# Five seven-product pairs in one more group of a fused linear-attention and SwiGLU kernel, batch 7's q in fewer early steps, and the last copy in another tile

## The chip, the cores and the metric

The kernel runs on one core of a Trainium2 chip. The core has a matrix engine (TensorE, in the profile PE, with its weight loads as PEld), a vector engine (VectorE, DVE), an engine for functions of single elements (ScalarE, ACT), a general one (GpSimd, POOL), and one that mostly starts transfers (SyncE, SP). They run side by side, each through its own list of instructions in order, and wait for each other through semaphores. The metric is the device time of one execution in microseconds (us): lower is better. Matmul results go to PSUM, which has eight banks of 128 partitions x 512 numbers of 32 bits; the kernel calls them pG (two), pV (three) and pX (three). Everything else on the chip lies in SBUF.

## The reference

q, k and v have 8 batches, 8 heads, 576 positions and 64 dimensions. The first half is linear attention, the second a SwiGLU block on its output x (4608 tokens of 512):

```python
def phi(x):
    return np.where(x > 0, x, np.exp(x) - 1.0) + 1.0
q_p, k_p = (phi(q), phi(k))
kv = np.einsum('bhsd,bhse->bhde', k_p, v)
z = np.sum(k_p, axis=2)
num = np.einsum('bhsd,bhde->bhse', q_p, kv)
den = np.einsum('bhsd,bhd->bhs', q_p, z)[..., None] + 1e-06
x = (num / den).transpose(0, 2, 1, 3).reshape(B * S, H * D)
g = x @ w_gate                       # 512 to 1536
out = (g / (1 + np.exp(-g)) * (x @ w_val)) @ w_out   # and back to 512
```

## The kernel before, in words

**Groups.** A batch is 9 units of 64 tokens, so there are 72 units; a group is 8 units, 512 tokens, and there are 9 groups, 0 to 8. Since a group has 8 units and a batch 9, group g needs the end of batch g-1 and most of batch g. Group 0 and the attention of batches 0 to 2 run in a part of their own ahead of line 800. From there the work of groups 1 to 8 is recorded as a list of operations: each call of op(engine, cost, function, reads, writes) appends one. At the end the line numbers of a long string, steps, say in which order the recorded operations are issued. The order was found beforehand by a planner from the costs given to op and the named reads and writes; the kernel itself only plays it back. So the order on each engine is fixed, and semaphores are set from the tiles and banks that instructions touch.

**Attention, for each batch b.** phis (line 913) makes phi(x) as min(exp(x), max(x, 0) + 1): for k and for q, plus_1_all (line 132) writes max + 1 of the whole tile into kp or qp on VectorE, ScalarE puts exp into a tile ek or eq (exp_, line 122), and least (line 138) takes the minimum with it. Two table loads of ScalarE stand around it. casts copies v; kv_prd (line 926, in ORDER the letter J) multiplies k and v; chain (line 882) spreads the sums z over all partitions (zb, zb_copy) and calls norm (line 888), which normalizes q in qp in place, in chunks of units: s3_prod, s3_half, s3_reduce, s3_recip and s3_scale on VectorE (lines 224 to 250). Then tr transposes the chunk by a DMA into qT. S3 and SCALE say which chunks are done right after chain, S3L and SCALEL which are left to the next group's first layer. x_prd (line 932, the letter M) makes x of the next group from qT and the k-v product, in four banks that x_copy moves to SBUF.

**First layer of group g** (layer_1, line 1028). The 1536 hidden columns are 12 blocks. A plain block is c_chunk (line 822): 16 matmuls for two blocks (8 for gate, 8 for value over four slices of x, each 128x128 by 128x512), a silu on ScalarE and one multiplication on VectorE for each block. A pair, pair_prd (line 837), makes two blocks by Winograd's form of Strassen's scheme: 7 products of half-size matrices instead of 8, each of four matmuls with 256 columns (prd_1, line 342). It needs sums of weights, made once (wl_sum, the list WL says in which group), and sums of x, made for each group (x_sums). Between the products ScalarE copies three partial results (keep_1, line 365) and applies silu twice (silu_1, line 368), and VectorE does two multiplications and an addition from PSUM (lines 371 and 857) and one multiplication in SBUF (line 866). NP says how many pairs a group has: 0, 3, 3, 5, 5, 6, 6, 6 for groups 1 to 8. With four pairs or more, layer_1 interleaves two pairs and fills the places between their products with what the second layer of the group before left over (fill) and with the chunks of the plain blocks.

**Second layer** (layer_2, line 1099) uses the same 7-product scheme over the whole layer: products 1 to 7 for two token halves (prd, line 439; h_sum, line 419, on VectorE makes the sums). The string ORDER[g] gives the products in order; what stands behind the bar | is left to the next group's first layer. keep, fin and copy_half bring the results to osb, and put sends them out. In the last group, the last product's bank pX_1 is emptied by two engines, partitions 0 to 63 by VectorE and 64 to 127 by ScalarE (lines 1000 and 1002), both into the tile osb_3, and two transfers follow.

Of the kernel before, what the change touches and what calls it, by code (L numbers as in the profile page):

```python
# [9 lines left out]
AF = mybir.ActivationFunctionType  # L10
# [7 lines left out]
def kernel(  # L18
# [215 lines left out]
    def s3_reduce(b, c):  # L234
        j0, j1 = js_of(c)
        nc.vector.tensor_reduce(out=den[:, HL * j0:HL * j1],
                                in_=prod[:, 0:j1 - j0, :].rearrange("p j (l d) -> p (j l) d", d=D)[:, :, 0:D // 2],
                                axis=AX.X, op=ALU.add)
# [581 lines left out]
    NP = {1: 0, 2: 3, 3: 3, 4: 5, 5: 5, 6: 6, 7: 6, 8: 6}  # L820
# [60 lines left out]

    def chain(b):
        op("PE", 0.25, lambda: zb(b), [f"R{b % 2}.{hh}" for hh in range(2)], ["X0"])
        for hh in range(2):
            op("ACT", 0.3, lambda hh=hh: zb_copy(b, hh), ["X0"], [f"zbc{hh}"])
        norm(b, S3[b], SCALE[b])

    def norm(b, chunks, scales):
        dens = []
        for (j0, j1) in chunks:  # L890
            (c, n, js) = ((j0, j1), j1 - j0, list(range(j0, j1)))
            dens.append(f"den{c}")
            op("DVE", 0.07 + 0.147 * n, lambda c=c: s3_prod(b, c), rqp(b, js) + ["zbc0", "zbc1"], ["prod"])
            op("DVE", 0.07 + 0.069 * n, lambda c=c: s3_half(c), ["prod"], ["prod"])
            op("DVE", 0.08 + 0.143 * n, lambda c=c: s3_reduce(b, c), ["prod"], [f"den{c}"])
# [16 lines left out]

    def phis(b):
        op("ACT", 1.28, lambda: nc.scalar.preload_act_table_set("exp_and_others"), [], ["table"])
        for (src, e, dst, w) in ((k16, ek, kp, [["kp1.0"], ["kp1.1"]]), (q16, eq, qp, [rqp(b, lps=[0]), rqp(b, lps=[1])])):
            a = "k" if src is k16 else "q"
            we = [["ek0.0", "ek0.1"], ["ek1.0", "ek1.1"]] if src is k16 else [["eq0"], ["eq1"]]
# [6 lines left out]
    KVB = {**{b: ["X2", "V2"] for b in range(B)}, 2: ["X0", "X1"], 7: ["X1", "V0"], 6: ["X1", "V0"], 5: ["X1", "V0"]}  # L924
# [34 lines left out]
    def l2_prd(g, n, tt, fs=tuple(range(HF)), done=True):  # L959
# [37 lines left out]
        if n == 4:  # L997
            if last and tt:
# [3 lines left out]
                op("ACT", 0.3, lambda: nc.scalar.activation(out=o2[hi, 0:HD], in_=x[hi, 0:HD], func=AF.Copy, bias=0.0,  # L1002
                                                            scale=1.0 / SC), [nm(x)], [f"o{2 + tt}.0b"])
                op("SP", 0.06, lambda: put_1(g, tt, 1, 0, 0, nc.sync), [f"o{2 + tt}.0a"], [])
                op("ACT", 0.06, lambda: put_1(g, tt, 1, 0, 1, nc.scalar), [f"o{2 + tt}.0b"], [])
# [14 lines left out]
    def put_1(g, tt, th, ch, e, eng):  # L1020
        (b, j) = units(g)[2 * (2 * th + tt) + e]
        eng.dma_start(out=out[S * b:S * b + S, HD * ch:HD * ch + HD].rearrange("(c j) f -> j c f", j=J)[j],  # L1022
                      in_=osb[2 * th + tt][C * e:C * e + C, HD * ch:HD * ch + HD])
# [73 lines left out]
    WL = {2: [(1, 1, 1), (2, 0, 1)], 3: [(2, 1, 1), (3, 0, 1)], 4: [(3, 1, 1)]}  # L1097
# [45 lines left out]
    ORDER[99] = ""; S3[7], SCALE[7], S3L[7], SCALEL[7] = ((0, 1),), ((0, 1),), ((1, 5), (5, 9)), ((1, 3), (3, 6), (6, 9)); S3[6], SCALE[6], S3L[6], SCALEL[6] = ((0, 2),), ((0, 2),), ((2, 5), (5, 9)), ((2, 5), (5, 9),); S3[5], SCALE[5], S3L[5], SCALEL[5] = ((0, 5),), ((0, 3), (3, 5)), ((5, 9),), ((5, 9),)  # L1143

    ORDER.update({g: "10 11 20 21 60 61 50 51 70 71 M 30 31 | 41 40 J" for g in (3,4)})
# [3 lines left out]
    def program():  # L1149
# [21 lines left out]
        0 1 4 14 15 9 17 18 10 5 20 21 23 6 24 26 27 16 29 2 19 30 32 8 3 33 35 36 7 22 38 28 41 25 39 40 42 31  # L1171
        34 44 171 45 43 47 37 63 49 46 64 48 66 12 50 67 69 105 65 70 51 11 72 52 73 75 68 71 13 76 106 78 74 77
        79 53 81 82 80 84 83 54 85 107 87 55 88 86 90 89 91 119 93 92 94 96 114 95 97 56 99 98 100 102 57 101
        103 113 127 108 58 104 129 128 109 131 115 110 133 59 130 135 117 132 60 134 137 111 139 136 125 138 112
        120 141 143 118 140 145 142 116 122 147 146 150 124 148 126 144 153 151 162 121 154 165 123 156 155 168
        61 163 176 157 158 177 62 149 169 172 152 164 179 167 170 166 159 178 160 181 197 161 180 199 342 183
        200 182 343 198 202 184 204 201 206 173 203 207 185 209 205 208 211 210 214 186 215 174 212 218 220 219
        222 175 221 216 223 213 225 187 224 227 217 229 226 188 230 228 285 232 231 189 234 236 235 237 233 240
        242 238 241 245 243 246 239 248 190 247 250 244 249 252 251 253 276 255 193 254 257 256 259 277 258 191
        260 262 261 264 192 194 267 265 268 263 271 266 273 269 272 274 270 284 298 275 300 278 280 299 302 288  # L1180
        281 279 304 282 301 306 286 303 308 305 283 310 296 309 307 312 287 311 314 289 313 293 316 290 318 317
        291 315 321 319 294 324 297 333 322 326 292 336 325 195 334 339 328 329 327 347 196 320 504 323 335 348
        340 330 337 350 341 338 332 349 352 331 368 353 370 354 369 371 355 373 372 375 356 295 377 357 378 380
        379 351 382 381 358 385 386 376 383 389 344 387 391 393 374 392 394 390 384 396 359 398 395 388 400 399
        360 401 397 403 456 402 405 404 407 345 408 406 411 409 413 346 412 361 416 410 414 417 419 415 418 421
        364 423 422 424 420 426 425 447 428 362 427 430 429 431 448 363 365 433 432 435 438 436 439 434 442 437
        444 440 443 445 441 455 469 446 471 449 451 470 473 459 452 450 475 474 472 477 453 457 479 476 454 478
        481 467 480 462 483 460 485 458 482 487 484 486 464 461 489 498 488 491 468 463 501 490 499 492 494 505
        493 502 507 465 506 510 495 508 512 466 496 497 515 366 517 516 523 513 367 500 503 509 518 525 514 519
        511 527 529 524 528 540 526 542 541 545 543 531 547 546 629 550 530 552 548 551 554 532 553 556 544 558  # L1190
        555 561 557 559 563 562 549 566 560 564 568 567 570 565 569 533 572 571 574 520 577 620 579 575 578 582
        580 573 584 534 583 586 588 585 587 590 576 593 535 595 581 594 591 598 589 600 596 599 602 601 592 603
        536 606 521 608 611 604 537 607 612 522 609 605 614 613 615 617 597 616 618 610 628 622 642 619 644 623
        643 624 646 632 621 648 625 647 645 650 627 637 652 649 626 654 651 653 635 656 633 658 700 657 660 655
        538 630 662 659 539 661 671 663 701 640 631 674 664 666 672 677 667 665 673 679 675 678 702 682 676 680
        684 668 639 681 669 687 670 689 634 688 703 694 641 685 636 690 696 686 691 683 698 638 706 695 715 699
        697 717 704 716 720 708 722 721 725 718 705 707 727 726 723 729 728 709 731 730 719 733 736 710 732 734
        738 737 724 741 735 739 743 742 745 711 747 740 744 746 749 748 752 795 754 750 753 757 796 759 755 758
        761 712 760 763 762 751 765 713 768 764 770 756 769 714 773 766 692 775 871 777 776 778 767 781 771 774
        783 779 782 786 693 784 787 789 809 790 780 788 792 791 793 785 803 815 772 794 817 797 816 819 799 810  # L1200
        798 821 800 820 818 823 801 805 825 822 827 824 802 826 812 829 804 831 872 828 806 833 830 807 832 835
        834 844 873 836 808 847 837 845 839 850 840 838 846 852 848 874 851 849 855 853 842 857 856 841 854 875
        814 860 843 862 876 861 813 865 863 867 877 864 858 869 811 866 859 882 891 868 870 893 892 880 896 883
        898 897 901 894 884 903 902 899 905 904 907 885 906 895 909 912 878 908 914 913 917 900 879 881 910 919
        918 921 915 920 923 922 911 925 928 886 924 926 930 929 916 933 931 927 935 934 937 887 932 939 936 938
        941 940 888 944 942 946 945 949 889 947 951 890 950 953 979 952 955 954 943 957 980 960 956 958 962 961
        965 948 959 968 963 969 966 971 970 972 967 974 964 973 975 977 981 978 976 989 990 991 992 993 983 996
        982 998 1000 997 1002 984 1004 987 999 1011 995 1003 1001 1013 985 1015 988 1014 1012 986 1017 994 1047
        1019 1016 1018 1007 1006 1021 1020 1005 1023 1022 1008 1026 1024 1028 1010 1027 1025 1009 1031 1029 1033
        1048 1032 1030 1049 1036 1034 1038 1037 1035 1050 1041 1039 1051 1043 1042 1040 1052 1045 1044 1060 1046  # L1210
        1062 1061 1065 1063 1067 1066 1053 1070 1064 1068 1072 1071 1074 1069 1076 1073 1075 1078 1077 1054 1081
# [45 lines left out]
```

## Time and profile before

Time: 295.01 us, the median of 3 runs (294.98 to 295.08). The profiled execution spans 293.5 us, with the full TensorE clock throughout.

| what | busy us | share of the span |
|---|---|---|
| TensorE matmuls | 286.2 | 98% |
| TensorE weight loads | 213.0 | 73% |
| VectorE | 258.6 | 88% |
| ScalarE | 236.2 | 80% |
| GpSimd | 45.1 | 15% |

Busy time is the union of an engine's instructions, so that two which overlap by a few hundredths are counted once. A share is an average over the span: the first 20 us, in which data come in and batch 0 is prepared, and the last 4 us, in which results go out, look unlike the rest. In the profile's slices, each digit is the busy share in tenths of a fortieth of the span (7.3 us). A row of a group gives the line, the engine, the operation and its tiles, how often it came, its busy time and the mean of one in ns. A row of the timeline begins with start and duration; in brackets stands how long the engine was idle before it and who ended that.

Groups 1 to 8 run from 52.4 to 289.6 us. A table by stretches, cut where each group's second layer begins, is shown in the prediction.

### The profile page before, as it was taken

The page shows a single profiled execution, that of the slowest core. Times are in us where ns is not written, and L with a number is a line of the kernel's source. Part 1 is how long each engine was busy: PE and PEld are TensorE (multiplying, and loading weights), DVE is VectorE, ACT ScalarE, POOL GpSimd, SP SyncE. Part 2 cuts the span into 40 slices and gives each one's busy share as a digit, 9 for nine tenths or more (in the row PEclk, how much of TensorE's full clock was granted, in tenths as well). Part 3 has the DMA queues.
Part 4 walks back from the last instruction along what each step waited for, and adds up shares of the span by engine and source line. Part 5 has one row for each costly group of instructions (what it writes and reads, how often), then busy time and mean ns, then how long its engine had stood idle before and what let it go on. Part 6 is the DMA issues. An engine that isn't in the chain of part 4 may idle for free.

```text
span 293.5 us, 7371 instructions
## 1 busy us (share of the span) xinstructions
PE 286.2 (98%) x2939; PEld 213.0 (73%) x2939; DVE 258.6 (88%) x521; ACT 236.2 (80%) x406; POOL 45.1 (15%) x59
## 2 busy tenths in 40 slices
PE   7899999999999999999999999999999999999994
PEld 5644454444876687667888788878888888788883
DVE  4766789999999999999979999999999999957982
ACT  4873977993999588987999999999986689669841
POOL 8654436500111001010100111000000000000003
PEclk9999999999999999999999999999999999999999
DMA  7999999995398229853990749701430143033005
GB/s 211 193 196 200 205 208 208 191 229 85 63 175 186 49 54 152 183 75 63 137 179 21 107 65 249 68 3 44 101 65 9 44 109 69 0 68 79 0 2 143
DMA packets 41314, 32.92 MB, mean 112 GB/s; under 512 B 16432, under 2 KB 36592, under 8 KB 41280
## 3 DMA queue, kind: packets, MB, share of 16 engines
q0 software_dynamic: 20304, 18.62, 41.4%
q1 hardware_dynamic: 20736, 13.64, 21.3%
q8 instruction: 23, 0.38, 0.5%
q10 hardware_dynamic: 240, 0.20, 0.3%
q14 instruction: 11, 0.09, 0.1%
HBM read 37.75 MB, written 9.44 MB: 161 GB/s over the span
## 4 chain that ended last, share of the span: by engine, by line
PE 95%; DMA 2%; ACT 1%; issue 0%; DVE 0%; POOL 0%; POOLq 0%
PE pX L456 20%; PE pV L351 14%; PE pG L351 12%; PE pX L351 10%; PE pV L828 8%; PE pG L828 7%; PE pV L456 5%; PE pX L297 3%; PE pV L297 3%; DMA q<-in_q_dram 2%; PE pG L383 2%; PE pV L383 2%; PE pG L297 2%; PE pX L828 2%; PE pX L187 1%; PE pX L268 1%
## 5 line engine op out<-in xcount | busy, mean ns | idle before, releaser
L351 PEld LDWEIGHTS <-wl 128*128 128x128 f16 x414 | 40.2, 98 | 9.4
L456 PEld LDWEIGHTS <-hs 128*128 128x128 f16 x384 | 37.2, 98 | 5.1 <-issue 0.6
L456 PEld LDWEIGHTS <-hT 128*128 128x128 f16 x288 | 27.7, 98 | 5.0 <-DVE hs L425 0.4
L351 PEld LDWEIGHTS <-wg 128*128 128x128 f16 x272 | 26.4, 98 | 5.7
L456 PE MATMUL pX<-ws,hs 128*128 128x256 f16 x240 | 29.1, 273 | 0.0
L828 PE MATMUL pV<-xt,wv 128*128 128x512 f16 x104 | 28.3, 379 | 0.0
L368 ACT ACTIVATE ek<-eq 128x512 f16<-128x512 f32 x34 | 21.3, 625 | 5.1 <-DVE eq L857 5.0
L351 PE MATMUL pV<-xt,wg 128*128 128x256 f16 x168 | 23.9, 273 | 0.0
L368 ACT ACTIVATE ek<-pV 128x512 f16<-128x512 f32 x34 | 20.4, 599 | 3.3 <-PE pV L351 2.6
L828 PE MATMUL pG<-xt,wg 128*128 128x512 f16 x80 | 22.5, 379 | 0.0
L465 ACT ACTIVATE part<-pX 128x256 f32<-128x256 f32 x40 | 14.5, 386 | 6.9 <-PE pX L456 6.7
L351 PE MATMUL pX<-xs,wl 128*128 128x256 f16 x132 | 19.8, 273 | 0.0
L1022 POOL DMA_DIRECT2D out_dram<-osb x5 | 2.7, 541 | 110.5 <-DVE osb L472 110.5
L371 DVE SCALAR_TENSOR_TENSOR r<-pG,rr 128x512 f16<-128x512 f32 x20 | 13.8, 688 | 6.6 <-PE pG L351 6.4
L456 PE MATMUL pX<-wo,hT 128*128 128x256 f16 x138 | 18.2, 273 | 0.0
L374 DVE SCALAR_TENSOR_TENSOR hT<-pV,sil 128x512 f16<-128x512 f32 x26 | 17.5, 682 | 0.5 <-PE pV L828 0.4
L425 DVE TENSOR_TENSOR hs<-hT 128x512 f16<-128x512 f16 (+3 forms) x35 | 17.7, 514 | 0.1
L365 ACT ACTIVATE rr<-pX 128x512 f32<-128x512 f32 x27 | 15.9, 597 | 2.0 <-PE pX L351 1.9
L249 DVE TENSOR_TENSOR qp<-qp,rden 128x768 f16<-128x768 f16 (+3 forms) x19 | 17.2, 906 | 0.0
L828 PEld LDWEIGHTS <-wv 128*128 128x128 f16 x112 | 11.0, 98 | 8.5
L124 ACT ACTIVATE ek<-k 128x1152 f16<-128x1152 f16 x14 | 16.2, 1164 | 1.1 <-DMA k<-in_k_dram 1.0
L351 PE MATMUL pG<-xs,wl 128*128 128x256 f16 x100 | 16.9, 272 | 0.0
(190 smaller groups left out, 723.4 us busy)
## 6 DMA issues: line engine op xcount, KB each, us to landing
out_dram<-osb SPq DMA_DIRECT2D x64, 128.0 KB, 2.4
k<-in_k_dram POOLq DMA_DIRECT2D x7, 576.0 KB, 7.6
q<-in_q_dram POOLq DMA_DIRECT2D x7, 576.0 KB, 10.1
v<-in_v_dram POOLq DMA_DIRECT2D x7, 576.0 KB, 6.4
wg<-in_moe_w_gate_dram POOLq DMA_DIRECT2D x5, 256.0 KB, 9.3
wv<-in_moe_w_val_dram POOLq DMA_DIRECT2D x5, 256.0 KB, 9.9
wo<-in_moe_w_out_dram POOLq DMA_DIRECT2D x2, 512.0 KB, 15.1
ws<-in_k_dram SPq DMA_DIRECT2D x1, 576.0 KB, 3.8
```

Of the source, the lines that this page charges most:

```text
L124: nc.scalar.activation(out=e[:, s, :], in_=src[ix(b)][:, s, :], func=AF.Exp, bias=0.0, scale=1.0)
L249: nc.vector.tensor_tensor(out=qv, in0=qv, in1=rden[:, HL * j0:HL * j1].unsqueeze(2).to_broadcast([P, HL * (j1 - j0), D]), op=ALU.mult)
L297: nc.tensor.matmul(out=ps[:, :], lhsT=src[:, i, P * fb:P * fb + P], rhs=xT[i][g % 2][:, :], start=(i == 0), stop=(i == 3))
L351: nc.tensor.matmul(out=dst[:, HN * e:HN * e + HN], lhsT=lhs, rhs=rhs, start=(n in (1, 5) and e == 0 and c == 0), stop=(c == 1), skip_group ...
L365: nc.scalar.activation(out=dst, in_=halves(src), func=AF.Copy, bias=0.0, scale=scale)
L368: nc.scalar.activation(out=dst, in_=src, func=AF.Silu, bias=0.0, scale=1.0)
L371: nc.vector.scalar_tensor_tensor(out=dst, in0=halves(src), scalar=SC, in1=b, op0=ALU.mult, op1=op1)
L374: nc.vector.scalar_tensor_tensor(out=hT[:, fb, :], in0=pv[:, :], scalar=SC, in1=s[:, :], op0=ALU.mult, op1=ALU.mult)
L425: (eng or nc.vector).tensor_tensor(out=o, in0=a, in1=b, op=op)
L456: nc.tensor.matmul(out=(z if n in (2, 3, 5) else x)[:, 0:HD], lhsT=left(f), rhs=right(f), start=(i == 0 and fs[0] == 0 and (n in (1, 5) or ...
L465: nc.scalar.activation(out=part[:, 2 * i + tt, :], in_=(x if from_x else z)[:, 0:HD], func=AF.Copy, bias=0.0, scale=1.0 / SC)
L828: nc.tensor.matmul(out=dst[:, :], lhsT=src[:, i, P * fb:P * fb + P], rhs=xT[i][g % 2][:, :], start=(i == 0), stop=(i == 3))
```

## The change

It does four things.

1. Group 3 has five pairs instead of three. For that, four of the five late weight sums come in group 2 and one in group 3, group 2's second layer takes the order of groups 3 and 4 (M earlier, and 41 40 J behind the bar), batch 4's k-v product gets the banks X1 and V0 as the later ones have, and the normalization of batches 4 and 5 is cut into other chunks.
2. For batch 7, phis leaves out q's part on VectorE. ScalarE writes exp(q) straight into qp (exp_in), and norm calls q_fin, which makes max(q, 0) + 1 in place in q16 and takes the minimum of both into qp, for unit 0 in group 6 and for units 1 to 8 in group 7.
3. In the last group, ScalarE's copy of the last product goes into the tile part, and is sent from there, so that it doesn't share osb_3 with VectorE's.
4. The order of steps is planned anew.

HALF is a switch that stays on, so that the normalization's steps stay as they were. The diff, with the string of step numbers left out:

```diff
-    def s3_reduce(b, c):
+    def s3_reduce(b, c, d):
...
-    NP = {1: 0, 2: 3, 3: 3, 4: 5, 5: 5, 6: 6, 7: 6, 8: 6}
+    NP = {1: 0, 2: 3, 3: 5, 4: 5, 5: 5, 6: 6, 7: 6, 8: 6}
...
+    HALF = {0: 1}
...
     def norm(b, chunks, scales):
         dens = []
+        if b in LATE:
+            q_fin(b, chunks[0][0], chunks[-1][1])
...
+    LATE = {7: True}
+
+    def exp_in(b, lp):
+        nc.scalar.activation(out=qp[b % 2][:, :, P * lp:P * lp + P].rearrange("p j (s d) -> p s j d", d=D),
+                             in_=q16[ix(b)][:, 2 * lp:2 * lp + 2, :].rearrange("p s (j d) -> p s j d", d=D), func=AF.Exp, bias=0.0,
+                             scale=1.0)
+
+    def q_fin(b, j0, j1):
+        n, js = j1 - j0, list(range(j0, j1))
+        r = q16[ix(b)][:, :, D * j0:D * j1]
+        op("DVE", 0.08 + 0.067 * n, lambda: nc.vector.tensor_scalar(out=r, in0=r, scalar1=0.0, scalar2=1.0, op0=ALU.max, op1=ALU.add),
+           ["q16"], ["q16"])
+        d = qp[b % 2][:, j0:j1, :].rearrange("p j (s d) -> p j s d", d=D)
+        op("DVE", 0.08 + 0.134 * n, lambda: nc.vector.tensor_tensor(out=d, in0=d, in1=r.rearrange("p s (j d) -> p j s d", d=D), op=ALU.min),
+           ["q16"] + rqp(b, js), rqp(b, js))
...
             a = "k" if src is k16 else "q"
+            if a == "q" and b in LATE:
+                for lp in range(2):
+                    op("ACT", 1.07, lambda lp=lp: exp_in(b, lp), ["q16", "table"], w[lp])
+                continue
...
-    KVB = {**{b: ["X2", "V2"] for b in range(B)}, 2: ["X0", "X1"], 7: ["X1", "V0"], 6: ["X1", "V0"], 5: ["X1", "V0"]}
+    KVB = {**{b: ["X2", "V2"] for b in range(B)}, 2: ["X0", "X1"], 7: ["X1", "V0"], 6: ["X1", "V0"], 5: ["X1", "V0"], 4: ["X1", "V0"]}
...
-                op("ACT", 0.3, lambda: nc.scalar.activation(out=o2[hi, 0:HD], in_=x[hi, 0:HD], func=AF.Copy, bias=0.0,
-                                                            scale=1.0 / SC), [nm(x)], [f"o{2 + tt}.0b"])
+                op("ACT", 0.3, lambda: nc.scalar.activation(out=part[hi, 0, :], in_=x[hi, 0:HD], func=AF.Copy, bias=0.0,
+                                                            scale=1.0 / SC), [nm(x)], ["part00"])
                 op("SP", 0.06, lambda: put_1(g, tt, 1, 0, 0, nc.sync), [f"o{2 + tt}.0a"], [])
-                op("ACT", 0.06, lambda: put_1(g, tt, 1, 0, 1, nc.scalar), [f"o{2 + tt}.0b"], [])
+                op("ACT", 0.06, lambda: put_1(g, tt, 1, 0, 1, nc.scalar, part[hi, 0, :]), ["part00"], [])
...
-    WL = {2: [(1, 1, 1), (2, 0, 1)], 3: [(2, 1, 1), (3, 0, 1)], 4: [(3, 1, 1)]}
+    WL = {2: [(1, 1, 1), (2, 0, 1), (2, 1, 1), (3, 0, 1)], 3: [(3, 1, 1)]}
...
-    S3[5], SCALE[5], S3L[5], SCALEL[5] = ((0, 5),), ((0, 3), (3, 5)), ((5, 9),), ((5, 9),)
+    S3[5], SCALE[5], S3L[5], SCALEL[5] = ((0, 3),), ((0, 3),), ((3, 6), (6, 9)), ((3, 6), (6, 9))
+    S3[4], SCALE[4], S3L[4], SCALEL[4] = ((0, 5),), ((0, 3), (3, 5)), ((5, 9),), ((5, 9),)
...
-    ORDER.update({g: "10 11 20 21 60 61 50 51 70 71 M 30 31 | 41 40 J" for g in (3,4)})
+    ORDER.update({g: "10 11 20 21 60 61 50 51 70 71 M 30 31 | 41 40 J" for g in (2,3,4)})
```

## The prediction, as put on record

> **What bounds the kernel now.** I read the busy shares first, then the slices, then the chain that ended last.
>
> ```profile
> PE 286.2 (98%) x2939; PEld 213.0 (73%) x2939; DVE 258.6 (88%) x521; ACT 236.2 (80%) x406; POOL 45.1 (15%) x59
> PE   7899999999999999999999999999999999999994
> DVE  4766789999999999999979999999999999957982
> ACT  4873977993999588987999999999986689669841
> PE 95%; DMA 2%; ACT 1%; issue 0%; DVE 0%; POOL 0%; POOLq 0%
> ```
>
> TensorE (PE) is busy in all slices but the first and the last, and 95% of the chain is its own matmuls. The list of waits, asked for TensorE's matmuls from 52.4 us on, where group 1's first layer starts, is empty. A busy PE could still hide short waits, because the records of matmuls overlap. So I also compared the distances between their starts: four products of 128x256 take 0.435 us, four of 128x512 take 0.865 us, all through the groups, and only some 0.1 us is lost where 64-row matmuls stand between. So TensorE works without a pause from 19.6 to 289.6 us, and time leaves only where its work leaves or the 3.9 us after its end get shorter.
>
> But VectorE (DVE) shows 9 in most slices too. How near is it? I cut the run where each group's second layer starts its first product (74.10, 104.45 and so on: groups 1 to 7), so that each stretch holds layer 2 of one group and layer 1 of the next:
>
> ```profile
> core 0: us, PE busy (x) PEld busy (x) DVE busy (x) ACT busy (x) POOL busy (x), PEclk, DMA share, GB/s
> 74.10:104.45 30.35, 30.35 (x303) 22.08 (x302) 29.38 (x56) 25.38 (x46) 2.22 (x3) 1.00 0.71 121
> 104.45:134.85 30.40, 30.40 (x310) 22.16 (x309) 28.94 (x55) 26.32 (x46) 2.23 (x3) 1.00 0.66 119
> 134.85:164.50 29.65, 29.65 (x334) 24.56 (x333) 27.45 (x54) 28.64 (x52) 2.22 (x3) 1.00 0.56 92
> 164.50:194.10 29.60, 29.60 (x334) 24.57 (x333) 28.90 (x61) 28.73 (x52) 1.48 (x2) 1.00 0.71 115
> 194.10:222.15 28.05, 28.05 (x334) 24.47 (x333) 27.46 (x58) 26.85 (x50) 0.00 (x0) 1.00 0.27 58
> 222.15:250.55 28.40, 28.40 (x271) 24.78 (x269) 27.08 (x57) 21.32 (x43) 0.00 (x0) 1.00 0.27 57
> ```
>
> The first figure after the times is the length. The first two stretches hold groups with three pairs and last 30.4 us, the next two five pairs and 29.6 us. That is the worth of two pairs, measured in the same program. The DVE column is the other half: 97 to 98% in the two stretches from 164.50 to 222.15, still without a wait of TensorE.
>
> **What the Trainium skill says.** "Perfetto Trace Analysis", section "Identifying the Most-Contended Engine", takes the most occupied engine as the bound, but says that matmul busy time is no good measure; hence the start distances above. "VectorE: DVE Perf Modes", section "The perf-mode tier table", has a 16-bit tensor_scalar in SBUF at four elements a cycle and a tensor_tensor at two; 2048 elements take 693 and 1224 ns there. The trace agrees: tensor_scalar over 2304 elements (L133) takes 750 ns, tensor_tensor over 1536 (L425) 948 ns. "PSUM — Partial Sum Buffer", section "PSUM bank collisions raise a hardware error", says that ScalarE and VectorE may not read the same bank and 32-partition quadrant together; dependencies between any two accesses of a bank follow from it in a simple form. That bears on the last edit.
>
> **The change part by part.**
>
> Two more pairs in group 3. A pair replaces 16 matmuls of 512 columns by 28 of 256, in units of four: 4 x 0.865 = 3.46 us against 7 x 0.435 = 3.05 us, so 0.41 us less, 0.83 us for two. The stretches give 30.40 - 29.63 = 0.77 us. I take 0.77, since it holds the switches too. This lies wholly on the path. The price is on the other engines. On VectorE a pair has three steps of some 0.60 us from start to start and one of 0.34, where two plain blocks have two of 0.60:
>
> ```profile
> 158.82 0.42 DVE L866 TENSOR_TENSOR hT<-r,ek 128x512 f16<-128x512 f16 x1
> 159.16 0.68 DVE L857 TENSOR_TENSOR eq<-pV,rr 128x512 f32<-128x512 f32 x1
> 159.76 0.68 DVE L371 SCALAR_TENSOR_TENSOR hT<-pG,ek 128x512 f16<-128x512 f32 x1
> 160.37 0.69 DVE L371 SCALAR_TENSOR_TENSOR r<-pG,rr 128x512 f16<-128x512 f32 x1
> 160.98 0.95 DVE L249 TENSOR_TENSOR qp<-qp,rden 128x768 f16<-128x768 f16 x1
> ```
>
> (start, duration; the next starts before the end of the one ahead.) So 2.14 - 1.20 = 0.94 us more a pair, 1.9 us for two. On ScalarE (ACT), five steps take the place of two; some 0.52 us each from start to start, so 1.56 a pair, 3.1 us for two.
>
> Batch 7's q. Out of group 5's layer 2 go one tensor_scalar (L133, 0.75 us) and two minima (L140, 2 x 0.74), some 2.0 us from start to start. In come two in-place tensor_scalars (256 and 2048 elements) and two minima of the same sizes. No row shows these sizes; scaled from the 750 and 948 ns rows, with a floor of 0.2 us for the small ones, I get 0.2 + 0.68 + 0.28 + 1.22 = 2.4 us by duration, 2.1 from start to start. They cost the same and stand later: in the built order both maxima and the small minimum come in the stretch of group 6's first layer, the large minimum some forty instructions on, in group 7's. The two exps (L124, 1.17 us) now write a rearranged output; L161 writes in that pattern already and takes 1.175 us, so nothing is added. Their wait moves from VectorE to ScalarE: they must wait until batch 5's transposes have left qp. These are issued some 14 us of TensorE's work earlier and land within 7.7 us at worst (2.8 in the median), so I take it as free.
>
> The new splits, orders and weight sums (S3, SCALE, ORDER, WL, KVB). They move batch 4's late normalization into the next group, and group 2's last products beside group 3's first pairs, as groups 3 and 4 have it now. The built program has 10 more VectorE instructions: 4 for the pairs, 1 for q, 5 for one more chunk (three steps with a fixed part of about 0.1 us each, and two small ones of 0.17 and 0.28). I take 0.4 us.
>
> The sum for VectorE from 104.45 to 222.15: now 28.94 + 27.45 + 28.90 + 27.46 = 112.75 busy of 117.70 us. After: + 1.9 + 0.1 + 0.4 = 115.2 (a little less, since the large minimum goes out) in 117.70 - 0.77 = 116.9. That leaves 1.7 us or 1.5% idle over four groups, where the densest two have 2.2% now. ScalarE goes from 110.5 to 113.6 us, 97%, like its densest stretch now (28.73 of 29.60). So the work fits, barely. An in-order VectorE that is never ahead can't make up a late step: a bank is freed late and TensorE waits for it. With 0.7% less reserve than a stretch shown to be free of waits, I bound what is handed back from 0 to 0.8 us, and take 0.1, a single short wait of the kind that group 3 or 4 may now have.
>
> ScalarE's last copy. The end now:
>
> ```profile
> 288.79 0.82 PE L456 MATMUL pX<-ws,hT 128*128 128x256 f16 x6
> 289.65 0.42 DVE L1000 TENSOR_SCALAR osb<-pX 64x256 f32<-64x256 f32 x1 [0.23 <-PE pX L456]
> 290.10 0.38 ACT L1002 ACTIVATE osb<-pX 64x256 f32<-64x256 f32 x1 [1.38 <-DVE osb L1000]
> 290.51 0.47 ACTq L1022 DMA_DIRECT2D out_dram<-osb  x1
> ```
>
> The copy waits for VectorE's, not for TensorE; were this wait about the shared tile osb, another tile would save 290.10 - 289.65 = 0.45 us. But both also read the bank pX. In the built program the copy into part still waits on VectorE's semaphore, at the count of VectorE's last instruction (531 of 531; 521 of 521 before). Only a wait on an older output transfer is gone, and that one had ended. So I take 0 of 0.45.
>
> Sum: 295.01 - 0.77 + 0.1 = 294.3 us.
>
> **The rivals.** (a) VectorE, or the round between it and ScalarE, becomes the bound from group 3 on. For: 98.5% planned. Against: 97.8% over 57.65 us costs nothing now. If it needs the 2.2% idle of today's densest stretches, four groups take 115.2 / 0.978 = 117.8 us instead of 116.9: 0.9 us handed back, 295.1 us. (b) Slower: besides that, a longer wait appears at places that the new order makes tight, a transpose that lands after x of the next group is due (up to 7.7 us to landing seen; least reserve in the new order some 6 us of TensorE's work), or k of batch 5 coming late (7.6 us to landing, 10 us reserved). One such miss of 1.7 us on top of (a) gives 296. For it speaks only the 7.7; against, that no wait for a transpose or a late k shows on TensorE now. (c) The wait at the end is shortened all the same: 293.9.
>
> **How the numbers follow.** Forecast, 294.1 to 294.6: 0.60, four fifths of it below 294.42 (0.2% under 295.01). (a), 294.6 to 295.4: 0.23. (b): 0.10. (c): 0.07. Faster 0.55, same 0.35, slower 0.10. The range from 294.0 to 295.2 leaves out (b), the half of (c) and the edge of (a).
>
> **What would show it.** Right: the stretch that ends at group 3's second layer shrinks from 30.40 to 29.6 us; the others stay within 0.1; VectorE's share from there to group 6 rises to 98 to 99%; the list of TensorE's waits stays near empty; the last copy still starts some 0.45 us after TensorE's last product is out. Wrong: waits of TensorE for L371, L857, L365 or L425 in groups 3 to 5 that sum to over 0.5 us, or stretches of groups 4 and 5 longer than 29.65; a wait for a transpose; a last copy that starts together with VectorE's.

## The result, and the profile after

The changed kernel takes 296.5 us (median of 4 runs, 296.1 to 296.57) where the kernel before takes 295.04 in the same series: 1.0047 times as long, 95% interval 1.0029 to 1.0064. So the change costs some 1.4 us. The prediction, 294.3 and at most 295.2, was wrong; what came is its rival (b).

The page of the changed kernel: busy shares, the slices of TensorE and VectorE, and the chain that ended last.

```profile
PE 285.8 (97%) x2963; PEld 214.9 (73%) x2963; DVE 260.3 (88%) x531; ACT 239.7 (81%) x412; POOL 45.2 (15%) x59
PE   6899999999999999999899999999999999999994
DVE  4767789999999997999899999999999999957892
PE 89%; DMA 5%; ACT 4%; DVE 1%; issue 0%; POOL 0%; POOLq 0%; ACTq 0%
```

TensorE has a slice with an 8 in the middle, and the chain now runs 5% through transfers and 4% through ScalarE, where it had been TensorE's by 95%. The stretches, cut where the first product of each second layer starts (groups 2 to 6), show where:

```profile
core 0: us, PE busy (x) PEld busy (x) DVE busy (x) ACT busy (x) POOL busy (x), PEclk, DMA share, GB/s
104.13:133.98 29.85, 29.77 (x333) 24.50 (x332) 27.96 (x54) 28.66 (x51) 2.23 (x3) 1.00 0.50 89
133.98:165.29 31.31, 29.97 (x333) 24.38 (x332) 29.51 (x61) 29.11 (x53) 2.22 (x3) 1.00 0.63 111
165.29:195.18 29.89, 29.89 (x334) 24.45 (x333) 29.44 (x63) 29.09 (x52) 1.48 (x2) 1.00 0.60 114
195.18:223.12 27.94, 27.94 (x333) 24.57 (x332) 27.49 (x61) 26.74 (x50) 0.00 (x0) 1.00 0.32 58
```

The stretch with group 3's pairs went from 30.40 to 29.85 us, where 29.6 was predicted. The next one went from 29.65 to 31.31, of which 1.34 us are without TensorE work; the one after it from 29.60 to 29.89 with no gap at all. Two losses, then, of different kinds: the gap, and 0.2 to 0.3 us in each of these three stretches.

The first is in the timeline around it. Rows are start, duration, engine, line, operation, and in brackets the idle time before and who ended it:

```profile
131.72 3.74 SPq L255 DMA_TRANSPOSE qT<-qp  x2
133.12 0.74 POOL L99 DMA_DIRECT2D v<-in_v_dram  x1 [19.48 <-ACT vm L161]
140.63 0.30 PE L268 MATMUL pG<-qT,R 64*64 64x256 f16 x4
...
142.38 0.30 PE L268 MATMUL pG<-qT,R 64*64 64x256 f16 x4 [1.34 <-DMA qT<-qp]
```

and in the chain, there in order of time:

```profile
133.55 0.60 DVE qp L249
134.15 0.03 DVE hT L866
134.18 8.16 DMA qT<-qp
142.34 0.04 issue
142.38 0.30 PE pG L268 x4
```

Batch 4's units 0 to 4 are transposed in two chunks. The first, at 131.72, lands in 2.7 us. Then GpSimd starts the load of v of batch 5 (576 KB), and the second chunk, issued 1.06 us later, needs 8.16 us. It holds unit 3, which x of group 4 (units 5 to 8 of batch 3, then 0 to 3 of batch 4) needs at 142.38 - 1.34 = 141.04, 6.86 us after the issue. In the kernel before:

```profile
127.30 0.74 POOL L99 DMA_DIRECT2D v<-in_v_dram  x1 [13.95 <-ACT vm L161]
131.54 2.55 SPq L255 DMA_TRANSPOSE qT<-qp  x2
141.67 0.28 PE L268 MATMUL pG<-qT,R 64*64 64x256 f16 x4
```

There the two chunks were issued at 131.54 and 132.80 and took 2.7 and 2.8 us; v's load had landed by 132.87, and x needed unit 3 at 141.67, 8.9 us after the second issue. The Trainium skill, "DMA: Bandwidth & Descriptors", section "Issuing engines are not separate DMA queues", says that transfers of all issuing engines run on the same 16 DMA engines and interleave. This trace agrees, with 2.7 us for the chunk ahead of the load against 8.16 for the one behind it.

For the second loss I use the distances between the starts of the x products (L268) of one group and the next, which the wait list can't show. The distance from group g's x to the next holds g's first layer and g's second layer up to that x:

| kernel | x2 to x3 | x3 to x4 | x4 to x5 | x5 to x6 | sum | x1 to x8 |
|---|---|---|---|---|---|---|
| before | 30.35 | 29.10 | 29.66 | 29.61 | 118.72 | 202.99 |
| changed | 29.04 | 29.86 | 31.30 | 29.89 | 120.09 | 204.24 |

x of group 3 comes two products (1.31 us) earlier now, which moves time from the first distance into the second. Without the 1.34 us of the transpose, the sum is 118.75. From 118.72 before, with the predicted 0.77 less, it should be 117.95: the worth of the pairs isn't there.

The end, answering to the last lines of the prediction's profile:

```profile
290.65 0.42 DVE L1025 TENSOR_SCALAR osb<-pX 64x256 f32<-64x256 f32 x1 [0.23 <-PE pX L456]
291.10 0.38 ACT L1027 ACTIVATE part<-pX 64x256 f32<-64x256 f32 x1 [1.38 <-DVE osb L1025]
```

ScalarE's copy still starts 0.45 us after VectorE's.

### The profile page after: what moved, and what is told of

Same layout as the page of the kernel before. It is cut to its first block, busy times and chain, and to the rows that moved or that the text cites. A ratio compares the mean times of both kernels' runs of the same rounds, so it can differ in the third digit from the quotient of the medians.

```text
span 294.7 us, 7452 instructions
## 1 busy us (share of the span) xinstructions
PE 285.8 (97%) x2963; PEld 214.9 (73%) x2963; DVE 260.3 (88%) x531; ACT 239.7 (81%) x412; POOL 45.2 (15%) x59
## 4 chain that ended last, share of the span: by engine, by line
PE 89%; DMA 5%; ACT 4%; DVE 1%; issue 0%; POOL 0%; POOLq 0%; ACTq 0%
PE pX L456 18%; PE pV L351 15%; PE pG L351 13%; PE pX L351 8%; PE pV L828 6%; PE pV L456 5%; PE pG L828 5%; DMA qT<-qp 3%; PE pV L297 3%; PE pX L297 3%; DMA q<-in_q_dram 2%; PE pG L383 2%; PE pV L383 2%; PE pG L297 2%; PE pX L828 2%; PE pX L187 1%
## 5 line engine op out<-in xcount | busy, mean ns | idle before, releaser
L351 PEld LDWEIGHTS <-wg 128*128 128x128 f16 x288 | 27.8, 98 | 4.6
L351 PE MATMUL pV<-xt,wg 128*128 128x256 f16 x180 | 25.6, 273 | 0.0
L828 PE MATMUL pV<-xt,wv 128*128 128x512 f16 x84 | 22.4, 380 | 0.0
L371 DVE SCALAR_TENSOR_TENSOR r<-pG,rr 128x512 f16<-128x512 f32 x24 | 16.5, 689 | 6.3 <-PE pG L351 4.4
L351 PE MATMUL pG<-xs,wl 128*128 128x256 f16 x120 | 20.3, 273 | 0.0
L365 ACT ACTIVATE pV<-pG 128x512 f32<-128x512 f32 x24 | 14.0, 583 | 4.2 <-PE pG L351 3.6
L351 PE MATMUL pV<-xs,wl 128*128 128x256 f16 x114 | 16.7, 273 | 0.1
L371 DVE SCALAR_TENSOR_TENSOR hT<-pG,ek 128x512 f16<-128x512 f32 x24 | 16.3, 681 | 0.3 <-PE pG L351 0.3
L351 PEld LDWEIGHTS <-wv 128*128 128x128 f16 x144 | 14.1, 98 | 2.9
L351 PE MATMUL pX<-xs,wl 128*128 128x256 f16 x108 | 16.2, 273 | 0.0
```

Of the source, the lines that this page charges most:

```text
L351: nc.tensor.matmul(out=dst[:, HN * e:HN * e + HN], lhsT=lhs, rhs=rhs, start=(n in (1, 5) and e == 0 and c == 0), stop=(c == 1), skip_group ...
L365: nc.scalar.activation(out=dst, in_=halves(src), func=AF.Copy, bias=0.0, scale=scale)
L371: nc.vector.scalar_tensor_tensor(out=dst, in0=halves(src), scalar=SC, in1=b, op0=ALU.mult, op1=op1)
L828: nc.tensor.matmul(out=dst[:, :], lhsT=src[:, i, P * fb:P * fb + P], rhs=xT[i][g % 2][:, :], start=(i == 0), stop=(i == 3))
```

## The experiments

Ratios are to the kernel before, run on the same chip in the same series; 0.1% is 0.3 us.

**The late transpose, and the end.** Four kernels, the first two from the changed kernel, the others from the one before.

First: batch 4's chunks cut so that the early one holds all that x of group 4 needs.

```diff
-    SCALE[4] = ((0, 3), (3, 5))
+    SCALE[4] = ((0, 4), (4, 5))
```

> The changed kernel, with batch 4's first two normalization chunks cut as units 0-3 and 4 instead of 0-2 and 3-4; the same VectorE work, and all that group 4's x needs of batch 4 is in the first transpose, issued ahead of batch 5's v load. Theory A (the transpose of the second chunk, issued 1.1 us after the v load, lands 8.2 us later and holds TensorE 1.6 us at group 4's x): no wait for a transpose there, the stretch that ends at group 4's second layer 1.5 us shorter than the 31.5 us of the changed kernel, time 296.5 - 1.6 = 294.9. Theory B (VectorE and ScalarE, now full, are the bound, and the wait for the transpose only stands where another would): TensorE's wait moves to VectorE's or ScalarE's results in groups 3 and 4, time 296 or more.

295.30 us, 1.0002 (0.9993 to 1.0010). No wait for a transpose is left, and the distances sum to 118.82. The load still slows the second chunk (the smallest and the largest figure are the two chunks):

```profile
L255 SPq DMA_TRANSPOSE qT<-qp x2: 1168/1200/1233, 132.2 to 134.3; - x2
DMA to landing us min/median/max: 3.1/5.7/8.2
```

Second: the load of v of batch 5 (353 in the string of steps) issued later, behind the load of k of batch 6 (471).

```diff
-    446 444 353 436 448
+    446 444 436 448
...
-    490 495 471 462 505
+    490 495 471 353 462 505
```

> The changed kernel, with batch 5's v load put behind batch 6's k load in GpSimd's queue, so that it starts some 9 us later, after group 4's x; nothing else moves. Theory A: the transpose of batch 4's units 3-4 lands in some 2.8 us instead of 8.2, no wait at group 4's x, time 294.9. If the long landing comes from the transpose itself or from the output transfers, it still takes about 8 us and time stays at 296.5. Theory B: the transpose lands early, but time stays at 296 or more. A risk for all: v comes too late for group 5's copies of v; that would show as a wait of ScalarE for it.

295.29 us, 0.9999 (0.9990 to 1.0008), no wait, and the second chunk now lands within 4.8 us:

```profile
L255 SPq DMA_TRANSPOSE qT<-qp x2: 1192/1202/1212, 131.8 to 134.3; - x2
DMA to landing us min/median/max: 2.7/3.8/4.8
```

In the seven kernels further down that keep this later load and whose trace tells the landing, the second chunk lands in 2.4 to 3.4 us. The moved load slows another transpose instead, one issued at 149.62 that lands after 9.6 us, but TensorE doesn't wait for that one.

Two different cures, each bringing back 1.3 to 1.4 us (120.09 to 118.82 and 118.66 in the distances). One keeps the slow transfer and takes the need away, the other keeps the need and takes the load away; so the collision with the load makes the transpose slow, and the short reserve makes it cost time. What neither brings is the 0.77 us of the pairs. The second kernel is the base of the following runs, called "the base" below.

Third and fourth: the kernel before with the last copy in part alone, and with VectorE alone copying all 128 partitions.

```diff
-    nc.scalar.activation(out=o2[hi, 0:HD], in_=x[hi, 0:HD], ...)
+    nc.scalar.activation(out=part[hi, 0, :], in_=x[hi, 0:HD], ...)
```

> The kernel before, with ScalarE's last copy put into part, as in the change, and nothing else. As predicted: the copy still waits for VectorE's read of the same bank; it starts 0.45 us after VectorE's, time 295.0, a difference of 0. The rival: the shared tile was the reason, 294.6.

```diff
-    nc.vector.tensor_scalar(out=o2[lo, 0:HD], in0=x[lo, 0:HD], ...)
-    nc.scalar.activation(out=o2[hi, 0:HD], in_=x[hi, 0:HD], ...)
+    nc.vector.tensor_scalar(out=o2[:, 0:HD], in0=x[:, 0:HD], ...)
```

> The kernel before, with VectorE alone copying all 128 partitions of the last product (ScalarE's last copy left out, its transfer kept). If the end is set by the second copy, which waits for the first, ScalarE's transfer is issued 0.4 us earlier (290.1 instead of 290.5), time 294.6. If the end is set by VectorE's half or by the transfers of SyncE, no change, 295.0.

295.19 us, 0.9997 (0.9988 to 1.0005): nothing, with ScalarE's copy waiting for VectorE as before. And 295.08 us, 0.9992 (0.9985 to 0.9998): 0.24 us. In the fourth kernel the single copy of twice the partitions takes what one half took:

```profile
289.02 0.42 DVE L1000 TENSOR_SCALAR osb<-pX 128x256 f32<-128x256 f32 x1 [0.23 <-PE pX L456]
```

**Who eats the worth of the pairs?** Four kernels take work off VectorE or ScalarE; the last is a control on the kernel before.

```diff
     def s3_half(c):                 # VectorE, in the first, third and fourth; now_b holds b
+        if now_b[0] in (4, 5, 6):
+            return
     def s3_reduce(b, c, d):
+        d = 8 if b in (4, 5, 6) else d
     def vcast(b, lp):               # ScalarE, in the second, third and fourth
+        if b in (5, 6, 7):
+            return
```

> The changed kernel with v of batch 5 loaded later (295.29 us), and VectorE relieved: for batches 4, 5 and 6 the halving add of the normalization (L232) is left out and the reduction (L236) takes 8 products of each head in place of 32, so the denominators of these batches are not the reference's. That takes some 1.6 us a batch from VectorE, 5 us in all, in groups 3 to 5. If VectorE is what eats the worth of the two pairs, the late starts of TensorE in groups 3 to 5 (0.71 us) go and the time falls to 294.6. If ScalarE's chain of copies does it alone, the time stays at 295.3.

> The changed kernel with v of batch 5 loaded later (295.29 us), and ScalarE relieved: the two copies of v (L161, 1.17 us each) are left out for batches 5, 6 and 7, so these batches are computed with v of batch 4. That takes 2.3 us from ScalarE in each of groups 3, 4 and 5. If ScalarE is what eats the worth of the two pairs, the time falls to 294.6; if it is VectorE alone, it stays at 295.3. If each engine has to be late for the other to matter, both this run and the one with less for VectorE bring most of the 0.7 us.

> Both reliefs at once: the denominators of batches 4 to 6 and v of batches 5 to 7 as in the two runs before. If the round between the two engines eats the worth of the pairs, the full 0.71 us comes back: 294.6 us, and the four distances between the starts of the x products from group 2's to group 6's sum to 118.0 instead of 118.66. If they still sum to 118.6, the loss is elsewhere (the pairs themselves are worth less than 0.77, or the products on 64 rows cost more), and the time stays at 295.3.

> The kernel before with the same two reliefs (denominators of batches 4 to 6 and v of batches 5 to 7 not the reference's). It had no late start over 0.05 us of TensorE in groups 2 to 5, so if late starts are the whole story it stays at 295.0 to 295.1, within 0.1 us of before. If it falls as much as the changed kernel does, the reliefs shorten something else (the start of the normalization, or the tail), and say nothing on the pairs.

| kernel | us | ratio (95%) | sum of the four distances |
|---|---|---|---|
| base | 295.29 | 0.9999 (0.9990 to 1.0008) | 118.66 |
| less for VectorE | 295.17 | 0.9992 (0.9985 to 0.9999) | 118.52 |
| less for ScalarE | 295.22 | 1.0001 (0.9991 to 1.0010) | 118.61 |
| less for both | 294.87 | 0.9985 (0.9978 to 0.9992) | 118.48 |
| before, less for both | 295.47 | 1.0008 (1.0002 to 1.0015) | 118.81 |

Both reliefs together bring 0.4 us in time but only 0.18 us in the distances, where 0.7 was expected; the kernel before gains nothing (it came out 0.2 us slower). So work of these engines costs the changed kernel time and the kernel before none, but most of the loss stayed. Where? In the base a product starts late here (TensorE and ScalarE, start and duration):

```profile
121.22 0.60 PE L351 MATMUL pV<-xt,wl 128*128 128x256 f16 x4
121.90 0.60 PE L351 MATMUL pV<-xs,wl 128*128 128x256 f16 x4
...
121.27 0.58 ACT L365 ACTIVATE pV<-pV 128x512 f32<-128x512 f32 x1
```

From one product to the next it should be 0.44 us, and it is 0.68: the product at 121.90 overwrites the bank that ScalarE's copy reads until 121.85. A busy share doesn't see this, since the earlier product's record lasts 0.60. The reliefs lay later in the group, and in all three relieved kernels this distance is still 0.68 or 0.69.

The whole loss of the base can be placed in this way, product by product. TensorE starts late behind a copy of ScalarE (L365) at 121.90 (by 0.24 us), 154.84 (0.12), 181.57 (0.06) and 189.10 (0.11), behind VectorE's sums of x (L340) at 174.79 (0.12), and loses 0.10 us within the k-v product of group 4. That makes 0.75 us; the kernel before has a single late start in these groups, of 0.05. (Both lose 0.09 us more at each change to products on 64 rows.)

**Order or amount?** In the base ScalarE is never idle for more than 0.03 us from group 3's x (110.88) until 122.4. I put the steps that nobody needs at once behind the copies that TensorE waits for. The second kernel adds the single last copy.

```diff
 steps: ScalarE's 375, 361 (silu, zb_copy) behind 384 (copy); 567 behind 576; 763 behind 781
        VectorE's 363, 572, 768, which need them, behind 390, 578, 783
```

> The changed kernel with v of batch 5 loaded later (295.29 us), and three steps of ScalarE put behind the copies that TensorE waits for, with the VectorE steps that need them put later too; the work is the same. Group 3: the silu of the sums (L859) and the second copy of the denominators' bank (L887) go behind the copy of the first product (L847); group 4: the silu of the third pair behind the next pair's copy; group 5: the silu behind the copy that frees pG. If the worth of the pairs is eaten by the order of ScalarE's queue in the first 12 us of a group, where it has no idle time, the late starts of TensorE at 121.90 (0.24), 154.84 (0.12) and 189.10 (0.10 us) go, the four distances between the x products sum to 118.2 instead of 118.66, and the time falls to 294.8. If it is a matter of the sum of work of VectorE and ScalarE over the groups, the same time is lost at other places: 295.3.

> The same, and at the end VectorE alone copies all 128 partitions of the last product, as in the earlier run with one copy (0.24 us less there than the time of before in the same call). The candidate that is to beat both kernels: 294.8 less 0.25, 294.5 to 294.6, if the order explains the loss; 295.0 if it doesn't. The result is the reference's.

295.63 us, 1.0011 (1.0003 to 1.0019), and 295.20, 1.0000 (0.9991 to 1.0008). The late start at 121.90 is gone, and 4 us later there is another, this time for VectorE's step, which the moved normalization had pushed back:

```profile
125.52 0.60 PE L351 MATMUL pV<-xs,wv 128*128 128x256 f16 x4 [0.22 <-DVE r L371]
```

The distances sum to 118.95: worse. The third order change also took away its late start (189.10), and 0.20 us more were lost in the layer 2 that follows (9.59 instead of 9.39). This order moves the loss and doesn't cure it.

That doesn't clear the order as such. In the first 12 us after group 4's x, the kernel before is as full as the base after group 3's (the columns are those of the stretches above; the kernel before comes first):

```profile
141.43:153.43 12.00, 12.00 (x188) 10.44 (x188) 9.90 (x19) 11.82 (x25) 0.74 (x1) 1.00 1.07 177
110.88:122.88 12.00, 11.92 (x186) 10.22 (x186) 10.40 (x20) 11.71 (x24) 0.74 (x1) 1.00 1.00 171
```

ScalarE is busy for 11.8 and 11.7 of 12 us, and yet TensorE loses 0.05 us there and 0.24 here. One thing that differs is where the silu of the sums (ek<-eq) stands: behind the copy that frees the bank in the kernel before, ahead of it (at 121.27, above) in the base:

```profile
151.40 0.58 ACT L365 ACTIVATE pV<-pV 128x512 f32<-128x512 f32 x1
151.89 0.62 ACT L368 ACTIVATE ek<-eq 128x512 f16<-128x512 f32 x1
...
120.14 0.62 ACT L368 ACTIVATE ek<-eq 128x512 f16<-128x512 f32 x1
120.66 0.58 ACT L368 ACTIVATE ek<-pV 128x512 f16<-128x512 f32 x1
```

In group 5 of the kernel before and in group 4 of the base, too, the copy goes first and its product is on time; in group 5 of the base the silu goes first and the product is 0.06 us late. The run above moved this silu together with a copy of the denominators' bank and the normalization behind it. An order with the silu alone moved was not run, so how much of the loss another order could bring back is open.

**The part on q.** The base with batch 7's q as before, VectorE's one max over 2304 elements and two minima in place of the four small steps.

```diff
-    LATE = {7: True}
+    LATE = {}
```

> The changed kernel with v of batch 5 loaded later, and batch 7's q as in the kernel before: one max over all of q in group 5's second layer, exps into eq, and two minima where the changed kernel has its early max and min steps. If the part on q is worth nothing, as the prediction has it, the time stays at 295.3 within 0.1. If it takes work out of a full VectorE, it is 0.2 to 0.3 us slower, in the distance from group 5's x to group 6's or the next.

295.74 us, 1.0015 (1.0008 to 1.0021). The distance x5 to x6 is 30.29 instead of 29.89. The part on q is thus worth 0.40 us in the new kernel's order of steps and has no share in the loss.

**Less work where the group begins.** The base, without ScalarE's copies of the denominators' bank and VectorE's steps for the first chunk, batches 4 to 6; and the base with the single last copy.

```diff
     def zb_copy(b, hh):
+        if b in (4, 5, 6):
+            return
+    left_out = {4: (0, 5), 5: (0, 3), 6: (0, 2)}
     def s3_prod(b, c):              # s3_half and s3_reduce too
+        if left_out.get(b) == c:
+            return
```

> The changed kernel with v of batch 5 loaded later (295.29 us), and work of both engines left out where a five-pair group begins: for batches 4, 5 and 6 ScalarE's two copies of the denominators' bank (L887, 0.38 us each) and VectorE's three steps of the normalization's first chunk (L226, L232, L236; 2.0 us for batch 4, some 1.3 and 0.9 for 5 and 6). These batches' denominators are then not the reference's. The earlier reliefs took 1.2 and 2 us out of the same groups, but later than the first 12 us. If the loss is a matter of these first 12 us, in which neither engine has idle time, the late starts at 121.90, 154.84 and 189.10 go without coming back elsewhere, the four distances sum to 118.1 to 118.2 instead of 118.66, and the time falls by some 0.5 us to 294.8. If they sum to 118.5 or more, the place is not it.

> The changed kernel with v of batch 5 loaded later, the order of ScalarE's steps as the change has it, and VectorE alone copying all 128 partitions of the last product. The result is the reference's. From 0.9999 of the time of before and the 0.24 us that one copy brought to the kernel before, 0.9991, or 295.05 us where before has 295.3: as fast as the kernel before with one copy, so the five pairs in group 3 add nothing. If the pairs' worth were only hidden by the measurement, it would come out at 294.6.

294.75 us, 0.9987 (0.9980 to 0.9994), the distances at 118.51. The second, 294.97 us, 0.9991 (0.9983 to 1.0000), is what the kernel before reaches with one copy too, so the pairs add nothing measurable. In the first, the product is on time:

```profile
120.99 0.60 PE L361 MATMUL pV<-xt,wl 128*128 128x256 f16 x4
121.43 0.60 PE L361 MATMUL pV<-xs,wl 128*128 128x256 f16 x4
```

**Less in both places**, and its control on the kernel before: the work left out for both engines in the earlier round and in this one.

> The changed kernel with v of batch 5 loaded later, with the work of both earlier reliefs left out: where a five-pair group begins (both copies of the denominators' bank and the first chunk's three steps, batches 4 to 6) and later in it (the halving add, three quarters of the reduction in batches 4 to 6, the copies of v in batches 5 to 7). Denominators of batches 4 to 6 and v of batches 5 to 7 are not the reference's. With less at the beginning alone, TensorE's pair products were on time, but layer 2 came 0.3 us late; with less later alone, layer 2 was on time and the pairs came late. If the two engines are short of time over the whole of a five-pair group, both places are now on time, the four distances sum to 118.0 (the full 0.77 less than before's 118.72), and the time is 294.4 or less. If something else takes the gain, the distances stay at 118.4 or more.

> The kernel before with the same work left out (first chunks of batches 4, 5 and 6 as this kernel cuts them, halving adds, part of the reductions, copies of v of batches 5 to 7). If the two engines held nothing up before, the four distances stay at 118.5 to 118.7, and the gap to the changed kernel with the same reliefs is the worth of the two pairs without their price: 0.5 to 0.8 us. If before gains as much, the reliefs have nothing to do with the pairs.

295.09 us, 0.9996 (0.9982 to 1.0010), and 295.16, 0.9996 (0.9986 to 1.0006). The first one's times scatter, 294.05 to 296.92, and its profiled run lost 1.9 us before group 1; so only its distances are of use: 118.52, against 118.68 in the control. They miss the expected 118.0. Divided by layers (TensorE's time from start to start, us; a late start is counted with the product before it):

| kernel | layer 1 of group 3 | of group 4 | of group 5 | layer 2 after group 3's | group 4's | group 5's |
|---|---|---|---|---|---|---|
| before | 19.53 | 18.89 | 18.84 | - | 9.27 | 9.27 |
| base | 19.08 | 19.00 | 19.01 | 9.28 | 9.27 | 9.39 |
| less for both, later | 19.09 | 19.05 | 18.96 | 9.28 | 9.27 | 9.27 |
| less at the beginning | 18.84 | 18.92 | 18.95 | 9.38 | 9.50 | 9.39 |
| less in both places | 18.84 | 18.92 | 18.94 | 9.38 | 9.50 | 9.27 |
| before, less in both | 19.53 | 18.84 | 18.85 | - | 9.27 | 9.27 |

(Layer 2 columns are the products between one group's x and the next; before has two fewer of them after group 3's x.) Group 3's first layer falls by 0.45 us in the base, and by 0.69 with less at the beginning in both places. So 0.24 of the 0.77 us is eaten there by work of ScalarE and VectorE in the first 12 us. What comes back is lost again in the columns of layer 2, 0.10 us in group 3's and 0.23 in group 4's. With less in both places, VectorE is held up just ahead of that:

```profile
138.50 0.43 DVE L485 SCALAR_TENSOR_TENSOR osb<-pV,part 128x256 f32<-128x256 f32 x1 [0.45 <-ACT ek L124]
```

The product behind this step starts 0.10 us late at 139.31. From there VectorE has no idle time until its sums of x (L340 in the numbers of the base), and the first layer's product that needs them starts 0.23 us late at 146.31. The kernel with less at the beginning has the hold too, and both late starts; the base and the one with less for both, later, have neither the hold nor these late starts. So a hold of 0.45 us on a VectorE without reserve came out on TensorE in part 8 us later. What held it is open: the page names the exp of k, but this step waits for an earlier copy, for TensorE's product and for old output transfers, and in the base it starts in the midst of that exp.

## Why the prediction was wrong

**The bound: right.** But for the end, time left only where TensorE's work or its late starts did.

**The pairs' worth: right, for TensorE alone.** Group 3's first layer falls by 0.69 us once the other engines have room, and the second layers of groups 2 and 3 show the rest (8.06 + 9.28 us in the base, 9.37 + 8.07 before). In the changed kernel the stretch came to 29.85 and not to 29.6, since 0.24 us of it was lost behind ScalarE's copy.

**What failed first: the chance of rival (b).** The prediction had its two numbers side by side, up to 7.7 us to landing and a reserve of "some 6 us of TensorE's work", and gave it 0.10 because "no wait for a transpose or a late k shows on TensorE now". That absence was evidence for the old order, in which the reserve was 8.9 us and the load had landed. 8.16 us against 6.86 cost 1.34 us, nearly all of what separates the medians (1.46) and more than the growth from group 1's x to group 8's (204.24 - 202.99 = 1.25). It was a sum to be worked out, not a chance to be weighed: in the order of steps v's load (353) stands between the two transposes (368 and 370).

**What failed second: the term "handed back", 0.1 us.** Measured: 0.71 (118.66 against 117.95). The amount of VectorE's work was well foretold: 27.96 + 29.51 + 29.44 + 27.49 = 114.4 us busy where 115.2 was planned. The step that failed is the one from this amount to the time: from 97 to 98% without a wait in the old order, the prediction took it that a new order with 98.5% loses nearly nothing. But a share doesn't say which steps stand ahead of a copy that TensorE waits for. Group 3's stretch has VectorE at 94% (27.96 of 29.85 us) and ScalarE at 96% (28.66), less than the densest stretch of the kernel before (28.90 and 28.73 of 29.60 us, 98 and 97%), where no product started late, and it loses 0.24 us to one late copy. For the same reason rival (a), with 0.9 us, is near the measured 0.71 in size alone: it reckoned that VectorE needs 2.2% of idle time, and more of the loss lies behind ScalarE's copies (0.53 us) than behind VectorE (0.12).

The runs show that relief where a group begins brings the pairs of group 3 on time (0.24 us), that relief later removes two of group 5's late starts, and that one other order only moves the loss. They do not settle all of it: with less in both places 0.57 us of the 0.77 are still missing (118.52 against 117.95). The starts place them, 0.33 us after VectorE's hold, 0.19 behind two of ScalarE's copies (156.25 and 190.38) and some 0.1 in the k-v products. What makes the hold, and whether a better order would avoid all this, stays open.

**Batch 7's q: wrong by 0.40 us, in the change's favour.** The sizes were right (0.22, 0.63, 0.28 and 1.22 us measured, 0.2, 0.68, 0.28 and 1.22 predicted). But "the same and stand later" was costed at nothing, on a VectorE that was about to be full; moving 2 us out of its fullest stretch (29.44 of 29.89 us) was worth a fifth of that. exp_in's wait was free, as predicted.

**The last copy: right.** 0 of 0.45 us, with part alone as well. The Trainium skill's "PSUM — Partial Sum Buffer", section "PSUM bank collisions raise a hardware error", which the prediction read for this, forbids the same bank and partition quadrant together; the two copies have different partitions, and the trace shows one waiting for the other all the same, with separate tiles too, so that of what they share only the bank is left. One copy in place of the two gains 0.24 us.

## What to carry to other kernels

Before a new order, list for each transfer that an early consumer needs the time from issue to need and what other load is issued within a few us of it, and compare with the slowest landing seen, not the median. On an engine pair without idle time a gain elsewhere comes back only if the work that it adds has room where it falls, so look at what stands ahead of each copy that the bounding engine waits for, and not at the mean of a stretch. And judge a busy engine by the distances between the starts of its products: TensorE, busy in all but 0.08 us from group 2's second layer to group 5's in the base, lost 0.2 to 0.3 us a group (29.86 to 29.89 from x to x in the base, 29.61 to 29.66 in the five-pair groups before).

## What the runs showed of the hardware

- A transpose of one or two units landed after 8.2 us when a load of 576 KB had been issued about 1 us ahead of it from another engine's queue, in two kernels; in eight kernels without that load it took 2.4 to 4.8.
- A VectorE copy out of PSUM of 64 partitions x 256 and one of 128 x 256 both take 0.42 us.
- Four matmuls of 128x256 start 0.44 us after the four before them, while their record lasts 0.60: a start that is late by up to 0.12 us leaves no idle time in the profile, and one of 0.24 leaves 0.08.
- The time before group 1 differs between executions of kernels that are alike up to there: from the span's start to group 1's x it was 50.5 to 52.4 us over these profiles. Distances between marks inside the run are free of it. They agreed to 0.02 us among the kernels before that differ only at the end, and to 0.03 us between two kernels with the base's order (29.87 and 29.84 from x4 to x5).
